# A retention and two-layer MoE kernel: another order of the seven products in a turn, and sign factors that GpSimd no longer applies

## The chip, the cores and the metric

The kernel runs on one core of one Trainium2 chip. The metric is device time in microseconds (us) from a run's start to its end; lower is better. The core's engines are named as the profile names them: PE (TensorE's matmuls), PEld (its weight loads), DVE (VectorE), ACT (ScalarE), POOL (GpSimd) and SP (SyncE, which issues all DMAs here).

## The reference

```python
def _attn_ref(q, k, v):                      # 4 x 8 heads, 576 positions, 64 wide
    ...
    Dmat = np.where(rel >= 0, gamma[:, None, None] ** rel[None, :, :], 0.0)
    ret = scores * Dmat[None, :, :, :]
    return np.matmul(ret, v).astype(np.float32)

def _moe_ref(x, w1, w2, w3, w_out):          # 2304 tokens, 512 -> 1024 -> 512
    a = x @ w1
    b = x @ w2
    h = a * b @ w3
    return (h @ w_out).astype(np.float32)

def _moe2_ref(x, w_in, w_out, alpha):        # 512 -> 2048 -> 512
    h = x @ w_in
    g = np.maximum(h, 0.0) + alpha * np.minimum(h, 0.0)
    return (g @ w_out).astype(np.float32)

def reference(**kwargs):
    attn_out = _attn_ref(**attn_kwargs)
    x = np.ascontiguousarray(attn_out.transpose(0, 2, 1, 3)).reshape(B * S, H * D)
    x = _moe_ref(x=x, **moe_kwargs)
    return _moe2_ref(x=x, **moe2_kwargs)
```

## The kernel before, in words

The program has six stages that follow each other on PE. First comes the retention. Then **the AB stage** multiplies x by w1 and w2 and forms a*b; it has 24 groups (8 column chunks times 3 pairs of token blocks). **The fold** multiplies w3 by w_out, **the y stage** multiplies a*b by the folded weight, **the G stage** multiplies y by w_in and applies the activation (24 groups again), and **the blocks** multiply g by the last weight (9 blocks).

AB stage, G stage and blocks use Strassen's scheme in Winograd's form: a 2 by 2 block product takes seven products instead of eight. The methods `p1` to `p7` are these products. In a group each of them is six matmuls of 128x384 (L792), since every operand is held as a high and a low part and three of the four combinations are computed. A group owns three PSUM banks, b1, b2 and b3, and the products share them:

- `p1` writes b1, and ACT copies b1 to b2 (L815 in the AB stage, L1278 in the G stage). `p6` then adds to b2, and ACT reads b2 (L823; L1273 with the output `u`). `p7` adds to b2 again, and DVE reads it (L832; L1266 with the input `p`). `p4` adds to b2 for the last time, and DVE reads it (L837; L1257 on ACT and L1259 on DVE).
- `p5` writes b3, and ACT reads it (L819; L1273 with the output `p`). `p3` adds to b3, and DVE reads it (L843 and L844; L1266 with the input `u`, then L1267).
- `p2` adds to b1, and ACT reads it (L827; L1257, with L1259 on DVE).

So `p6` waits for a copy of ACT behind `p1`, `p7` for a copy of ACT behind `p6`, and `p4` for a read of DVE behind `p7`. To cover these waits a turn of the loop issues four products of its own group n and three (`p7`, `p4`, `p3`) of group n-1, which is called `before`. What lies between two products on the same bank covers the wait between them.

PE, ACT and SP take their instructions in the order of the program text. DVE and POOL are ordered by a scheduler at build time; work written under `soon()` gets a higher priority there. The three places in a turn called "a", "b" and "c" take side work: a step of the next operands is issued at each of them.

One such side work in the G stage is the preparation of w_out2 for the blocks (`Operands`, five pairs of rows of the weight, ten steps a pair, one step at each place). Its raw data is float64: two DMAs of 512 KB (`rawo`, L226) bring a pair, ACT converts (L94, L95), four DVE instructions finish it (L104 to L109). Step names: `fx fy` is ACT's part, `sx sy` DVE's, `gx gy` multiplies by the sign of alpha on POOL (L301), `t1 t3` are sums (L284 on POOL), `h1` to `h4` round the high part on ACT (L252), `l1` to `l4` take the low part on DVE (L259) and issue the DMA of the result (`wod`, L266), `x y` load the next pair's raw data. The same class also prepares three pairs in the AB stage, and there the signs have always been scalar operands of the instructions that read the values (L254 on ACT, L261 and L282 on DVE).

Of the kernel before, what the change touches and what calls it, by code (L numbers as in the profile page):

```python
# [12 lines left out]
ALU = mybir.AluOpType  # L13
# [3 lines left out]
P = 128  # L17
# [130 lines left out]
def retention_moe_kernel(ctx: ExitStack, tc, qk, kv, w_out1, w3t, w12, w_in, w_out2, alpha, c_row, c_pair, out):  # L148
# [61 lines left out]
    class Operands:  # L210
# [58 lines left out]
        def add(self, j, at, steps, ahead=None):  # L269
# [6 lines left out]

            late = not self.small
            sx, sy, sxy = (sg[:, x:x + 1], sg[:, y:y + 1], both[:, j:j + 1]) if late else (None, None, None)

            def less(out, a, b, sign=None):  # L280
                if sign is not None:
                    nc.vector.scalar_tensor_tensor(out=out, in0=a, scalar=sign, in1=b, op0=ALU.mult, op1=ALU.subtract)  # L282
                else:
                    (nc.vector if late else nc.gpsimd).tensor_tensor(out=out, in0=a, in1=b, op=ALU.subtract)  # L284

# [11 lines left out]

            def signed(i):
                a = w.ab[i][0]
                if not late:  # L300
                    nc.gpsimd.tensor_tensor(out=a, in0=a, in1=sg[:, i:i + 1].to_broadcast([P, 512]), op=ALU.mult)  # L301

            parts = {
                "gx": lambda: signed(x), "gy": lambda: signed(y),
                "fx": lambda: w._first(x), "fy": lambda: w._first(y),
# [494 lines left out]
    class AbGroup(Group):  # L800
# [33 lines left out]
        def p4(self):  # L834
            self.product(self.b2, "A22", "T4", False)
            with soon():
                nc.vector.tensor_tensor(out=self.f[:, 0], in0=self.b2, in1=self.f[:, 0], op=ALU.mult)  # L837

        def p3(self):
            self.product(self.b3, "S4", "B22", False)  # L840
            u = self.f[:, 1]
            with soon():
                nc.vector.tensor_tensor(out=u, in0=self.b3, in1=u, op=ALU.add)  # L843
                nc.vector.tensor_tensor(out=u, in0=u, in1=self.p5s, op=ALU.mult)  # L844
            later.append(self.spill)

# [73 lines left out]
    for j in range(PAIRS_IN_X):  # L920
        ops2.add(j, 7 * j, ("fx", "sx gx fy x", "sy gy y", "h1 t1", "l1 h2 t3", "l2 h3", "l3 h4", "l4"), j + 1 < PAIRS_IN_X)

# [52 lines left out]
    def do(n, pos):  # L975
        for run in todo.pop((n, pos), ()):
            run()

    before = None
    for n, (c, p) in enumerate(ab_order):  # L980
        g = AbGroup(p, c, n)
        flush()
        g.p1()
        g.p5()
        if before:
            before.p7()
        do(n, "a")
        flush()
        g.p6()
        g.p2()  # L990
        do(n, "b")
        flush()
        if before:
            before.p4()
            before.p3()
        do(n, "c")
        before = g
    before.p7()
    flush()
    before.p4()  # L1000
    flush()
    before.p3()
    flush()
# [444 lines left out]
    for m in range(PAIRS_IN_X, C1):  # L1448
        ops2.add(m, 10 * (m - PAIRS_IN_X), ("fx", "sx gx fy", "sy gy", "h1 t1", "l1 h2 t3", "l2 h3", "l3 h4", "l4", "x", "y"),
                 m + 1 < C1)  # L1450
# [29 lines left out]
    for n, (p, j) in enumerate(groups):  # L1480
# [3 lines left out]
        flush()  # L1484
        g.p1()
        g.p5()
        spot(n, "a")
        if last:
            some_of(make, 1)
        if before:  # L1490
            before.p7()
        flush()
        if first:
            some_of(make, 2)
        g.p6()
        if last:
# [15 lines left out]
        if before:  # L1512
            before.p4()
            if first:
                some_of(make, 2)
                if p + 1 < NP:
                    x_room(p + 1)
                    for o in range(KT):
                        for t in range(2):
                            nc.sync.dma_start(out=xs_of[p + 1][:, o, t], in_=x2d[2 * (p + 1) + t, o])  # L1520
            before.p3()
        if j == 5 and p + 1 < NP:
# [32 lines left out]
    blocks[0].ops[2]()  # L1555
    before.p4()
    for_sums("cells7")
    flush()
    before.p3()
    for_sums("cells8")  # L1560
# [114 lines left out]
```

## Time and profile before

| what | value |
|---|---|
| time, median of 3 runs | 780.08 us (779.30 to 780.43) |
| the profiled execution | 780.34 us, its span 778.6 us |
| PE busy | 750.1 us, 96% of the span |
| DVE busy | 638.2 us, 82% |
| ACT busy | 424.0 us, 54% |
| POOL busy | 59.9 us, 8% |
| mean granted clock of TensorE | 0.985 |

The span runs from the first to the last instruction of the profiled execution. Busy time is summed over the whole span, while the stages have different limits, so what a change in one stage is worth is read from PE's waits in that stage.

### The profile page before, as it was taken

The numbers are of one execution on the slowest core, as the hardware profiler recorded it, in microseconds if no ns is written. First come the engines' busy times: TensorE is split into PE (matmuls) and PEld (weight loads), VectorE is DVE, ScalarE is ACT, GpSimd is POOL, SyncE is SP. The second block draws the span as 40 slices with busy tenths as digits, with TensorE's granted clock in tenths as the row PEclk, the third lists the DMA queues.
The fourth block names the chain that finished last, engine by engine and source line by source line (L and its number), as shares of the span: only waits on it lengthen the run. The fifth ranks groups of instructions, "written<-read, shape, count | busy, mean of one in ns | idle before, by whom it ended". The sixth has DMA issues, their size and how long they took to land. (4 is left out here: it accounts for less than half of the span.)

```text
span 778.6 us, 13360 instructions
## 1 busy us (share of the span) xinstructions
PE 750.1 (96%) x4977; PEld 701.6 (90%) x4979; DVE 638.2 (82%) x1042; ACT 424.0 (54%) x750; POOL 59.9 (8%) x67
## 2 busy tenths in 40 slices
PE   8887899999999999999999989899999999999998
PEld 5676799999999888999999989899999888888887
DVE  4889987999799869999996669769777788887884
ACT  3555465666466546766765447456544444444442
POOL 1444100000000000000001211212300000000000
PEclk9789999999999999999999999999999999999999
DMA  9954125677657975596845986655999654444440
GB/s 340 391 175 199 57 72 175 223 250 227 223 189 230 396 284 205 195 358 236 285 183 194 343 326 238 244 193 191 349 369 352 216 158 142 133 128 141 133 129 28
DMA packets 106849, 173.26 MB, mean 223 GB/s; under 512 B 8096, under 2 KB 73888, under 8 KB 106784
## 3 DMA queue, kind: packets, MB, share of 16 engines
q1 hardware_dynamic: 106784, 172.40, 63.8%
q8 instruction: 39, 0.64, 0.3%
q14 instruction: 26, 0.21, 0.1%
HBM read 112.34 MB, written 60.03 MB: 221 GB/s over the span
## 5 line engine op out<-in xcount | busy, mean ns | idle before, releaser
L1203 PE MATMUL y<-yab,wa 128*128 128x384 f32 x576 | 100.0, 334 | 0.0
L1203 PEld LDWEIGHTS y<-yab,wa 128*128 128x128 f32 x576 | 99.9, 188 | 0.1
L1368 DVE TENSOR_TENSOR cells<-cells,cells 128x1024 fp32r<-128x1024 f32 x63 | 76.4, 1221 | 26.2 <-ACT cells L1362 26.0
L1387 PE MATMUL o<-wa,cells 128*128 128x512 f32 x288 | 76.6, 392 | 0.0
L1362 ACT CAST cells<-cells 128x1024 fp32r<-128x1024 f32 x63 | 65.0, 1052 | 7.5 <-DVE cells L1355 4.4
L1387 PEld LDWEIGHTS o<-wa,cells 128*128 128x128 f32 x288 | 51.4, 189 | 8.5
L792 PE MATMUL h<-xT,wa 128*128 128x384 f32 x288 | 55.8, 335 | 2.3 <-DVE g L1266 2.0
L792 PE MATMUL h<-xB,wa 128*128 128x384 f32 x288 | 57.4, 338 | 0.0
L1387 PE MATMUL o<-wop,cells 128*128 128x512 f32 x216 | 57.0, 392 | 0.2 <-DVE cells L1399 0.2
L792 PE MATMUL h<-xl,wa 128*128 128x384 f32 x288 | 54.9, 336 | 0.5 <-ACT h L815 0.5
L792 PEld LDWEIGHTS h<-xT,wa 128*128 128x128 f32 x288 | 50.3, 188 | 2.9 <-DVE g L1266 2.3
L792 PEld LDWEIGHTS h<-xl,wa 128*128 128x128 f32 x288 | 50.1, 188 | 1.5 <-ACT h L815 1.4
L792 PEld LDWEIGHTS h<-xB,wa 128*128 128x128 f32 x288 | 51.2, 190 | 0.0
L792 PE MATMUL h<-wa 128*128 128x384 f32 x264 | 49.7, 335 | 0.0
L792 PE MATMUL h<-xr,wa 128*128 128x384 f32 x240 | 45.7, 335 | 2.0 <-DVE xs L832 1.7
L1387 PEld LDWEIGHTS o<-wop,cells 128*128 128x128 f32 x216 | 39.4, 188 | 8.1 <-issue 0.3
L792 PEld LDWEIGHTS h<-wa 128*128 128x128 f32 x264 | 46.0, 188 | 0.3 <-ACT h L815 0.2
L301 POOL TENSOR_TENSOR a<-a,al 128x512 f32<-128x512 f32 x10 | 11.1, 1113 | 444.0 <-DVE a L109 444.0
L1389 PEld LDWEIGHTS o<-wa,cells 128*128 128x128 f32 x288 | 41.8, 190 | 3.5
L1389 PE MATMUL o<-wa,cells 128*128 128x256 f32 x288 | 44.5, 282 | 0.0
L792 PEld LDWEIGHTS h<-xr,wa 128*128 128x128 f32 x240 | 41.9, 188 | 2.6 <-DVE xs L832 2.1
L1259 DVE SCALAR_TENSOR_TENSOR g<-h,al,g 128x384 f32<-128x384 f32 x48 | 29.2, 611 | 14.1 <-ACT g L1257 12.0
(228 smaller groups left out, 1586.4 us busy)
## 6 DMA issues: line engine op xcount, KB each, us to landing
gd<-g SPq DMA_DIRECT2D x96, 192.0 KB, 4.1
cells<-gd SPq DMA_DIRECT2D x36, 512.0 KB, 6.0
abd<-xs SPq DMA_DIRECT2D x24, 384.0 KB, 3.6
yf<-abd SPq DMA_DIRECT2D x24, 384.0 KB, 6.0
rawi<-in_w_in_dram SPq DMA_DIRECT2D x16, 512.0 KB, 5.8
wod<-wo2u SPq DMA_DIRECT2D x28, 256.0 KB, 2.4
wa<-wod SPq DMA_DIRECT2D x12, 512.0 KB, 6.5
wod<-xs SPq DMA_DIRECT2D x21, 256.0 KB, 4.1
```

Of the source, the lines that this page charges most:

```text
L301: nc.gpsimd.tensor_tensor(out=a, in0=a, in1=sg[:, i:i + 1].to_broadcast([P, 512]), op=ALU.mult)
L792: nc.tensor.matmul(ps, a[:, x, ks], b[:, y, k], start=(fresh and n == 0), stop=(n == 5), skip_group_check=True)
L1203: nc.tensor.matmul(ys[o], wpc[c][a][:, oc], yab[u][:, bb, c % 2], start=(c == 0 and i == 0), stop=(c == C1 - 1 and i == 2))
L1259: nc.vector.scalar_tensor_tensor(out=g, in0=ps, scalar=sal[:, c], in1=g, op0=ALU.mult, op1=ALU.max)
L1362: nc.scalar.copy(h.bitcast(F32R), self.q[name])
L1368: nc.vector.tensor_tensor(out=l.bitcast(F32R), in0=q[name], in1=h, op=ALU.subtract)
L1387: nc.tensor.matmul(ps, h[:, k], w[k], start=(fresh and k == 0), stop=(k == C1 - 1), skip_group_check=True)
L1389: nc.tensor.matmul(ps[:, 256:], l[:, k], w[k][:, 0:256], start=False, stop=(k == C1 - 1), skip_group_check=True)
```

## The change

In AB stage and G stage a turn's order goes from p1, p5, p7, p6, p2, p4, p3 to p1, p7, p5, p3, p6, p2, p4, where p7, p3 and p4 are still those of the group before. The last group's three come as p7, p3, p4. In the AB stage the DMA that spills a group's result is issued behind p4 in place of p3. In the G stage's weight preparation POOL has no work any more: the sign goes as a scalar operand into the instructions of ACT and DVE that read the values, the sums go to DVE, and the raw data of the next pair is loaded one place sooner.

```diff
@@ -274,14 +274,13 @@
-            late = not self.small
-            sx, sy, sxy = (sg[:, x:x + 1], sg[:, y:y + 1], both[:, j:j + 1]) if late else (None, None, None)
+            sx, sy, sxy = sg[:, x:x + 1], sg[:, y:y + 1], both[:, j:j + 1]
 
             def less(out, a, b, sign=None):
                 if sign is not None:
                     nc.vector.scalar_tensor_tensor(out=out, in0=a, scalar=sign, in1=b, op0=ALU.mult, op1=ALU.subtract)
                 else:
-                    (nc.vector if late else nc.gpsimd).tensor_tensor(out=out, in0=a, in1=b, op=ALU.subtract)
+                    nc.vector.tensor_tensor(out=out, in0=a, in1=b, op=ALU.subtract)
@@ -295,13 +294,7 @@
-            def signed(i):
-                a = w.ab[i][0]
-                if not late:
-                    nc.gpsimd.tensor_tensor(out=a, in0=a, in1=sg[:, i:i + 1].to_broadcast([P, 512]), op=ALU.mult)
-
             parts = {
-                "gx": lambda: signed(x), "gy": lambda: signed(y),
                 "fx": lambda: w._first(x), "fy": lambda: w._first(y),
@@ -835,6 +828,7 @@
             self.product(self.b2, "A22", "T4", False)
             with soon():
                 nc.vector.tensor_tensor(out=self.f[:, 0], in0=self.b2, in1=self.f[:, 0], op=ALU.mult)
+            later.append(self.spill)
@@ -842,7 +836,6 @@
                 nc.vector.tensor_tensor(out=u, in0=u, in1=self.p5s, op=ALU.mult)
-            later.append(self.spill)
@@ -981,25 +974,26 @@
         g.p1()
-        g.p5()
         if before:
             before.p7()
+        g.p5()
         do(n, "a")
         flush()
+        if before:
+            before.p3()
         g.p6()
         g.p2()
         do(n, "b")
         flush()
         if before:
             before.p4()
-            before.p3()
         do(n, "c")
         before = g
     before.p7()
     flush()
+    before.p3()
+    flush()
     before.p4()
-    flush()
-    before.p3()
@@ -1446,7 +1440,7 @@
-        ops2.add(m, 10 * (m - PAIRS_IN_X), ("fx", "sx gx fy", "sy gy", "h1 t1", "l1 h2 t3", "l2 h3", "l3 h4", "l4", "x", "y"),
+        ops2.add(m, 10 * (m - PAIRS_IN_X), ("fx", "sx fy", "sy", "h1 t1", "l1 h2 t3", "l2 h3", "l3 h4", "l4 x", "y", ""),
                  m + 1 < C1)
@@ -1483,15 +1477,17 @@
         g.p1()
+        if before:
+            before.p7()
         g.p5()
         spot(n, "a")
...
-        if before:
-            before.p7()
         flush()
         if first:
             some_of(make, 2)
+        if before:
+            before.p3()
         g.p6()
...
-            before.p3()
@@ -1553,10 +1548,10 @@
-    before.p4()
+    before.p3()
     for_sums("cells7")
     flush()
-    before.p3()
+    before.p4()
```

The program order of PE in turn 10 of the G stage, before; `h10_0`, `h10_1` and `h10_2` are b1, b2 and b3 of group 10, and `h9_...` those of group 9.

```order
L792 MATMUL h10_0_5201<-xB11_1_4844,wa_63 128x384 x6
L792 MATMUL h10_2_5203<-xT1_1_4962,wu1_1_4248 128x384 x6
L792 MATMUL h9_1_5115<-xT3_1_5057,wa_63 128x384 x6
L792 MATMUL h10_1_5202<-xT2_1_4983,wu1_1_4248 128x384 x6
L792 MATMUL h10_0_5201<-xB21_1_5001,wa_63 128x384 x6
L792 MATMUL h9_1_5115<-xT4_1_5060,wa_63 128x384 x6
L792 MATMUL h9_2_5116<-xB22_1_5092,wa_63 128x384 x6
```

The same turn now (the file is seven lines shorter here, so L792 is L785).

```order
L785 MATMUL h10_0_5195<-xB11_1_4841,wa_63 128x384 x6
L785 MATMUL h9_1_5111<-xT3_1_5053,wa_63 128x384 x6
L785 MATMUL h10_2_5197<-xT1_1_4968,wu1_1_4248 128x384 x6
L785 MATMUL h9_2_5112<-xB22_1_5098,wa_63 128x384 x6
L785 MATMUL h10_1_5196<-xT2_1_4989,wu1_1_4248 128x384 x6
L785 MATMUL h10_0_5195<-xB21_1_5009,wa_63 128x384 x6
L785 MATMUL h9_1_5111<-xT4_1_5056,wa_63 128x384 x6
```

Between p7 and p4 on `h9_1` there were two products and now there are four; between p1 (`h10_0`, first row) and p6 (`h10_1`) there were two and now there are three; between p6 of one turn and p7 of the next there were five and now there are three.

The program order of DVE at the end of the AB stage, before; `h22_1` is b2 of group 22, `h23_1` and `h23_2` are b2 and b3 of group 23, the last one; L104 to L123 prepare the fold's weights.

```order
L837 TENSOR_TENSOR xs_94<-h22_1_2719,xs_94 128x384
L105 TENSOR_SCALAR a11_2826<-a11_2826 128x512
L843 TENSOR_TENSOR xs_94<-h22_2_2720,xs_94 128x384
L107 SCALAR_TENSOR_TENSOR a11_2826<-raww11_2643,a11_2826 128x512
L123 TENSOR_TENSOR xl_1107<-a10_2785,xl_1107 128x512
L844 TENSOR_TENSOR xs_94<-xs_94 128x384
L832 TENSOR_TENSOR xs_94<-h23_1_2792,xs_94 128x384
```

The same place now (L832 is L825 and L837 is L830).

```order
L830 TENSOR_TENSOR xs_94<-h22_1_2719,xs_94 128x384
L107 SCALAR_TENSOR_TENSOR a11_2826<-raww11_2643,a11_2826 128x512
L123 TENSOR_TENSOR xl_1107<-a10_2785,xl_1107 128x512
L104 TENSOR_SCALAR a12_2921<-a12_2921 128x512
L825 TENSOR_TENSOR xs_94<-h23_1_2792,xs_94 128x384
```

The read behind p7 of group 23 still stands behind the preparation of two weights, but no longer behind p3's reads of group 22, which now come before p4's.

SP's queue at the end of turn 3 and in turn 4 of the G stage, before.

```order
L266 DMA wod4_84<-wo2u4_3_4632 128x512
L266 DMA wod6_86<-wo2u4_3_4632 128x512
L1242 DMA gd1_0_4503<-g2_4671 128x384
L1242 DMA gd0_1_4514<-g2_4681 128x384
L1232 DMA wv3_2_4685<-wud3_2_3866 128x1024
L1232 DMA wv3_3_4687<-wud3_3_3968 128x1024
L226 DMA rawo8_4689<-in_w_out2_dram 128x512
L226 DMA rawo9_4709<-in_w_out2_dram 128x512
```

The same place now.

```order
L266 DMA wod4_84<-wo2u4_3_4640 128x512
L266 DMA wod6_86<-wo2u4_3_4640 128x512
L226 DMA rawo8_4673<-in_w_out2_dram 128x512
L1236 DMA gd1_0_4513<-g2_4681 128x384
L1226 DMA wv3_2_4685<-wud3_2_3866 128x1024
L1226 DMA wv3_3_4687<-wud3_3_3968 128x1024
L226 DMA rawo9_4689<-in_w_out2_dram 128x512
```

The first raw load now goes ahead of one store of g and of two fetches of 512 KB; the second still follows them, a place sooner than before.

## Rows read from the trace of the kernel before

**Rows 1.** PE's waits: who waited for whom, us in total, times, longest

```profile
PE h L792 <- ACT h L1278: 3.0, 3, 1.8
PE h L792 <- DVE g L1266: 2.0, 1, 2.0
PE h L792 <- DVE xs L832: 1.7, 1, 1.7
PE h L792 <- ACT h L815: 0.7, 2, 0.5
```

**Rows 2.** PE's timeline, starts and ends of the two stages: start, us, instruction

```profile
91.75 4.35 PE L792 MATMUL h<-wa 128*128 128x384 f32 x24
...
271.05 2.92 PE L1043 MATMUL pw<-wa 128*128 128x512 f32 x12
...
414.48 1.20 PE L792 MATMUL h<-xB,wa 128*128 128x384 f32 x6
415.52 2.24 PE L792 MATMUL h<-xT,wa 128*128 128x384 f32 x12
...
595.92 0.39 PE L1414 MATMUL o<-wa,cells 128*128 128x512 f32 x1
```

**Rows 3.** PE's timeline, turns 6 and 7 of the G stage

```profile
457.56 1.31 PE L792 MATMUL h<-xT,wa 128*128 128x384 f32 x6 [0.27 <-ACT u L1273]
460.71 1.31 PE L792 MATMUL h<-xT,wv 128*128 128x384 f32 x6 [1.84 <-ACT h L1278]
...
466.03 2.25 PE L792 MATMUL h<-xT,wv 128*128 128x384 f32 x12
469.11 1.33 PE L792 MATMUL h<-xT,wv 128*128 128x384 f32 x6 [0.84 <-ACT h L1278]
```

**Rows 4.** Timelines of SP and of ACT, turns 4 to 7 of the G stage

```profile
447.74 1.81 SPq L226 DMA_DIRECT2D rawo<-in_w_out_dram  x2
...
455.80 0.66 ACT L94 ACTIVATE a<-rawo 128x512 f32<-128x512 f32 x1 [5.13 <-DMA rawo<-in_w_out_dram]
...
467.07 0.62 ACT L252 CAST wo2u<-a 128x512 fp32r<-128x512 f32 x1 [3.38 <-POOL a L301]
```

**Rows 5.** Timelines of DVE, PE and ACT, turn 10 of the G stage

```profile
490.25 1.01 DVE L630 TENSOR_TENSOR t_T<-xs 128x768 f32<-128x768 f32 x1 [1.74 <-DMA xs<-x2d]
...
495.57 1.31 PE L792 MATMUL h<-xT,wa 128*128 128x384 f32 x6 [2.01 <-DVE g L1266]
...
492.60 0.58 ACT L1273 ACTIVATE u<-h,al 128x384 f32<-128x384 f32 x1 [1.20 <-PE h L792]
```

**Rows 6.** Stretches: PE, PEld, DVE, ACT, POOL busy, clock, DMA share, GB/s

```profile
473.40:488.20 14.80, 14.80 (x86) 14.54 (x86) 14.71 (x25) 10.46 (x19) 0.00 (x0) 1.00 0.93 315
496.80:500.20 3.40, 3.40 (x13) 3.40 (x12) 2.23 (x4) 1.63 (x3) 2.74 (x4) 0.50 0.51 193
246.00:282.00 36.00, 34.26 (x183) 32.02 (x182) 26.49 (x53) 16.95 (x33) 0.00 (x0) 1.00 1.02 382
```

**Rows 7.** Timelines of PE and DVE at the end of the AB stage

```profile
265.89 1.21 PE L792 MATMUL h<-xr,wa 128*128 128x384 f32 x6
268.84 1.32 PE L792 MATMUL h<-xr,wa 128*128 128x384 f32 x6 [1.74 <-DVE xs L832]
...
268.24 0.55 DVE L832 TENSOR_TENSOR xs<-h,xs 128x384 f32<-128x384 f32 x1
```

**Rows 8.** Groups of DVE's instructions: count, busy us, mean ns, idle before

```profile
L282 DVE SCALAR_TENSOR_TENSOR xs<-xs,al 128x256 f32<-128x256 f32 x9 | 3.9, 479 | 0.0
L1267 DVE SCALAR_TENSOR_TENSOR g<-g,al 128x384 f32<-128x384 f32 x47 | 31.8, 677 | 0.6
```

**Rows 9.** Timelines of ACT, DVE and PE in the fold

```profile
281.84 0.66 ACT L94 ACTIVATE a<-raww 128x512 f32<-128x512 f32 x1 [8.15 <-DMA raww<-in_w3t_dram]
...
307.53 0.69 DVE L123 TENSOR_TENSOR wa<-a,wa 128x512 fp32r<-128x512 f32 x1
...
309.18 5.60 PE L1043 MATMUL pw<-wa 128*128 128x512 f32 x24
```

More of the change, by code (lines that the diff above doesn't have):

```diff
@@ L920, in retention_moe_kernel @@
     for j in range(PAIRS_IN_X):
-        ops2.add(j, 7 * j, ("fx", "sx gx fy x", "sy gy y", "h1 t1", "l1 h2 t3", "l2 h3", "l3 h4", "l4"), j + 1 < PAIRS_IN_X)
+        ops2.add(j, 7 * j, ("fx", "sx fy x", "sy y", "h1 t1", "l1 h2 t3", "l2 h3", "l3 h4", "l4"), j + 1 < PAIRS_IN_X)
     ab_order = [(0, 0), (1, 0), (0, 1), (1, 1), (0, 2), (1, 2)]
```

## The prediction

> **What bounds the kernel now.** PE is busy for 96% of the span, so the first view is the list of what PE waited for, and the question is what part of it lies in the two stages whose order changes. [rows 1] has the waits with a name there: in the G stage 3.0 us for ACT's copy b1 to b2 and 2.0 us for DVE's read behind p7, in the AB stage 1.7 us for DVE's read behind p7 and 0.7 us for ACT's copy. They are short, but a wait costs more than its gap: in [rows 3] the product that starts at 457.56 is followed by one that starts at 460.71, 3.15 us later, of which 1.84 is the gap and 1.04 the product; the other 0.27 is the drain before and the slower first matmul behind.
>
> So the second view is the length of each stage against its products. A product of six matmuls takes 1.04 us from start to start (414.48 to 415.52 in [rows 2]). The AB stage has 168 of them, 174.7 us, and lasts from 91.75 to 271.05, 179.3 us: 4.6 us are lost, 0.6 of them to two single matmuls that mark banks (0.17 us each and a restart). Of the other 4.0 the wait at the stage's end takes 2.0 [rows 7]: p4 of the last group starts at 268.84, 2.95 us behind p7's start, and its first matmul is slow by 0.1. The G stage has 166 products from 414.48 to 595.92: 181.4 us against 172.6, so 8.8 us are lost. Of these the named gaps are 5.3 (with 0.27 for ACT's `u`, [rows 3]) and five restarts 1.35; for 3.4 us the clock was granted at half [rows 6], which costs some 1.6; the remaining 0.5 are waits too short for the list. From all this the change can gain 4.0 + 8.8 = 12.8 us at most.
>
> The third view says why these waits end late. Turn 5's side work stood on a raw load: SP issued both loads at 447.74 and ACT's L94 ran at 455.80, after 5.13 us of idling [rows 4]; PE's waits at 457.3 and 458.9 are for ACT instructions queued behind it [rows 3]. In turn 7 ACT idled 3.38 us for POOL's sign product before L252 [rows 4], and the copy for PE stood behind that (0.84 us, [rows 3]). In turn 10 DVE stood on a DMA for 1.74 us [rows 5], its read behind p7 came late, and PE waited 2.01 us.
>
> **The change part by part.** *The order.* Each wait is hidden by what lies between the two products on a bank. p1 to p6 (ACT) goes from two products to three, 2.1 to 3.1 us; p7 to p4 (DVE) from two to four, 2.1 to 4.2 us; p6 to p7 (ACT) falls from five to three, 5.2 to 3.1 us. What falls is still enough where ACT is not held up: the `u` read takes 0.58 us and starts when PE releases it [rows 5]. PE issues the same 168 products a stage, so the edit itself costs nothing. In the AB stage the short waits in mid-stage, 4.0 - 2.0 = 2.0 us, are each below a product, and one product more covers them: 2.0 us gained. At its end the order p7, p3, p4 puts one product, 1.04 us, into the wait of 2.0; the read L832 starts at 268.24 [rows 7], and it still stands behind two weights' preparation, so I leave its time alone: 1.0 gained. The AB stage gives 3.0 us. The spill behind p4 waits for one DVE instruction where it waited for two, and frees the same queue of SP no later.
>
> *Raw loads a place sooner, no POOL.* A place is a third of a turn, some 2.4 us. The first load of turn 4 leaves SP ahead of two fetches of 512 KB too. So ACT's 5.13 us of idling in turn 5 falls below 2.7. The `u` read ended some 5.4 us behind its product (five products, 5.2, and PE still waited 0.27, [rows 3]); it now ends at most 3.0 behind, and three products, 3.1, cover that. In turn 7 there is no POOL step to wait for, and ACT's 3.38 us go. The four G waits for ACT (0.27, 1.84, 0.84 [rows 3], and the third of the 3.0 us in [rows 1], 0.3) go, with their restarts: 4.4 us. The wait of turn 10 needed 2.1 + 2.3 = 4.4 us behind p7; the new cover is 4.2 minus what DVE's order adds, so I leave 0.5 of its 2.3 us. The half clock fell 1.2 us after this wait; a gain of 1.6 us hangs on it. The waits too short to name (0.5) go. Sum for the G stage: 4.4 + 1.8 + 1.6 + 0.5 = 8.3, less 0.2 for a new short wait somewhere: 8.1 us.
>
> *What is added.* DVE gets 20 sums; 15 take a scalar, 0.48 us each in the AB stage's copy of this step [rows 8], and the other five no more: 9.6 us at most in 187 us. Against that, the second step of the activation, L1267, runs 0.60 to 0.62 us when alone and 0.677 on average [rows 8], which gives back up to 3 us. DVE's lag falls on p7 to p4, where the cover doubled, and on g's stores, which nobody waits for soon. ACT's 20 instructions with a scale cost some 0.05 us more each, nothing on PE.
>
> A rule of the Trainium skill speaks to this (SBUF — State Buffer, "Who interferes with whom"): a VectorE instruction with two SBUF inputs and a GpSimd instruction that reads SBUF exclude each other for a whole instruction. L1267 has two such inputs, and its mean above 0.62 agrees. By the rule more of DVE's work would be freed than these 3 us.
>
> On the clock, [rows 6] shows 0.50 granted, 1.2 GHz, for 3.4 us right behind turn 10's wait. Yet the wait of 1.74 us at the AB stage's end [rows 7] brought no fall: its stretch has 1.00, 2.4 GHz [rows 6]. The Trainium skill (TensorE: Matmul & The Clock Gate, "What's actually happening") has the clock follow TensorE's recent activity, so that fewer waits mean fewer falls; by it the 1.6 us are safe, by the rows alone they are only likely.
>
> **Sum.** 3.0 + 8.1 = 11.1 us. The profiled execution took 780.34 us, 1.7 outside its span and 0.26 above the median of 780.08. From the median: 769.0 us.
>
> **Rivals.**
>
> *The fold takes the AB gain back.* From 246 to 282 the DMA engines are full, share 1.02 at 382 GB/s [rows 6], and the fold's weight preparation starts with a raw load that lands at 281.8, after ACT idled 8.15 us [rows 9]. DVE then works without a break, and the low part for piece 22 (L123, 307.53 to 308.22) is ready 1.4 us before PE needs it, 0.45 us into the row of 309.18 [rows 9]. If DMA does not move ahead with PE, the 3.0 us become 1.4, and the time 770.6. Against it: the full stretch begins with fetches tied to turns that come 2 us sooner. The Trainium skill's ceiling near 436 GB/s (DMA: Bandwidth & Descriptors, "Where 436 GB/s comes from") is a little above the row's 382.
>
> *p7 waits.* If DMA is so full in turns 4 and 5 that the raw load lands no sooner, the `u` read ends 5.4 us behind its product, and with three products of cover p7 waits 2.3 us; the copy's wait in turn 6 (1.84 and a restart, 2.1) loses one product by its longer cover and keeps 1.1. With a restart each that is 3.9 us more than forecast, 772.9; if the clock falls there instead, 774.5.
>
> *DVE becomes the bound: slower.* In turns 8 and 9 DVE is busy 14.71 of 14.80 us [rows 6]. If the sums push DVE's lag past the cover, ACT's `wo2u` steps wait for DVE in order, and p6 and p7 wait behind ACT. To undo 11.1 us each of the five pairs must cost PE 2.2 us beyond the free 3.1 - 0.7 = 2.4 us, so DVE must fall 4.6 us behind within a pair; the sums add 1.9 a pair. At a lag of 6 us a pair the time is 780 + 5 x 1.4 = 787. The decisive point is 4.6 us.
>
> *No gain.* The blocks could be paced by DVE and ACT, and hand a late G stage's time back. Against it, PE hardly waits there: none of the waits in [rows 1] lies behind the G stage. It gives 777 to 780.
>
> **Chances.** Forecast (767.3 to 770) 0.62; fold 0.13; p7 waits 0.17; no gain 0.04; slower 0.04. The low end is all 12.8 us, 767.3. The range to 774 takes in the first three. One measurement can tell some 0.2%, 1.6 us, from no change: faster by more than that 0.93, within it 0.03, slower 0.04.
>
> **What would show it.** Right: PE's waits for L1278, L1266 and L815 nearly gone, one of 0.7 to 1.0 us for L832 at the AB stage's end, the G stage's 166 products in 173 to 174 us, no POOL row and no half clock in it. Wrong: a PE wait for L1273 `u` or L823 (the cover that shrank), PE waiting in the fold for L123, or ACT idling for DVE before `wo2u` in each pair.

## The result, and the profile after

The changed kernel takes 773.35 us (median of eight runs, 770.70 to 776.43) against 779.92 us for the kernel before (776.64 to 780.62). The ratio is 0.9916, 95% interval 0.9897 to 0.9935: faster by 6.6 us where 11.1 were forecast, inside the range and above the forecast's own case (767.3 to 770). Its profiled execution took 770.70 us, the lowest of the eight runs, its span 768.9.

What PE waited for from the AB stage to the end of the G stage, in the changed kernel (us in total, times, longest); it answers to [rows 1]:

```profile
PE h L785 <- ACT h L808: 1.4, 3, 0.8
PE h L785 <- DVE xs L825: 0.6, 1, 0.6
PE h L785 <- DVE g L1260: 0.5, 1, 0.5
PE pw L1037 <- DVE wa L123: 0.3, 1, 0.3
```

The reader is to see three things. The 3.0 us for ACT's copy in the G stage (L1278 before, L1272 now) have no row any more, and of the 2.0 us for DVE's read behind p7 there 0.5 are left. The wait at the AB stage's end fell from 1.7 to 0.6. But the wait for ACT's copy in the AB stage (L815 before, L808 now), which the change was forecast to cover, doubled from 0.7 to 1.4 us, and a wait in the fold is new.

PE's timeline at the stages' ends, as in [rows 2] and [rows 7] (start, us, instruction, idle before and its releaser):

```profile
89.53 4.32 PE L785 MATMUL h<-wa 128*128 128x384 f32 x24
...
142.94 2.35 PE L785 MATMUL h<-xr,wa 128*128 128x384 f32 x12 [0.76 <-ACT h L808]
...
267.20 1.32 PE L785 MATMUL h<-xr,wa 128*128 128x384 f32 x6 [0.57 <-DVE xs L825]
268.37 2.93 PE L1037 MATMUL pw<-wa 128*128 128x512 f32 x12
...
307.40 5.27 PE L1037 MATMUL pw<-wa 128*128 128x512 f32 x22 [0.27 <-DVE wa L123]
...
412.66 1.20 PE L785 MATMUL h<-xB,wa 128*128 128x384 f32 x6
...
562.64 1.31 PE L785 MATMUL h<-xT,wu 128*128 128x384 f32 x6 [0.51 <-DVE g L1260]
...
586.67 0.39 PE L1408 MATMUL o<-wa,cells 128*128 128x512 f32 x1
```

The AB stage lasts from 89.53 to 268.37, 178.84 us (179.30 before, [rows 2]), and the G stage from 412.66 to 586.67, 174.01 us (181.44 before). Between them the fold and the y stage got 0.86 us longer. The AB stage also starts 2.2 us sooner than in [rows 2], though the retention ahead of it is the same program: in the profiles of this study it takes 89.2 to 92.4 us whatever the kernel. How much of the scatter between unprofiled runs comes from there isn't shown. So stages are compared by their own lengths here, from the first matmul of one to the first of the next.

The G stage as one stretch, first of the kernel before, then of the changed one (columns as in [rows 6]):

```profile
414.40:595.90 181.50, 176.23 (x998) 174.06 (x997) 138.65 (x231) 99.28 (x183) 28.93 (x30) 0.99 0.81 284
```

```profile
412.60:586.70 174.10, 173.48 (x999) 172.61 (x998) 142.72 (x251) 100.90 (x183) 0.00 (x0) 1.00 0.86 295
```

POOL's 28.93 us are gone, DVE has 4.1 us more, and there is no stretch at half clock (1.00 against 0.99). What the raw loads did, in ACT's timeline of turns 5 and 6, to be read beside [rows 4]:

```profile
449.88 0.66 ACT L94 ACTIVATE a<-rawo 128x512 f32<-128x512 f32 x1
...
454.39 0.67 ACT L94 ACTIVATE a<-rawo 128x512 f32<-128x512 f32 x1 [1.43 <-DMA rawo<-in_w_out_dram]
```

The first load no longer stops ACT, the second stops it for 1.43 us, where one load stopped it for 5.13 before.

### The profile page after: what moved, and what is told of

Same layout as the page of the kernel before. It is cut to its first block, busy times and chain, and to the rows that moved or that the text cites. A ratio compares the mean times of both kernels' runs of the same rounds, so it can differ in the third digit from the quotient of the medians.

```text
span 768.9 us, 13332 instructions
## 1 busy us (share of the span) xinstructions
PE 746.5 (97%) x4977; PEld 698.2 (91%) x4979; DVE 642.9 (84%) x1062; ACT 425.7 (55%) x750; POOL 31.4 (4%) x37
## 4 chain that ended last, share of the span: by engine, by line
PE 70%; DVE 15%; DMA 10%; issue 2%; ACT 2%; SPq 1%; DVEq 0%; ACTq 0%
PE h L785 30%; PE o L1381 15%; PE y L1197 13%; PE o L1383 8%; DMA wod<-xs 3%; DMA wv<-wud 2%; PE o L442 1%; DVE a L107 1%; DMA raww<-in_w3t_dram 1%; DVE heads_l L395 1%; DVE wa L549 1%; DVE a L109 1%; PE sc L391 1%; DVE a L104 1%; DVE a L105 1%
## 5 line engine op out<-in xcount | busy, mean ns | idle before, releaser
L785 PE MATMUL h<-xB,wa 128*128 128x384 f32 x288 | 57.9, 335 | 0.1
L785 PE MATMUL h<-xl,wa 128*128 128x384 f32 x288 | 56.2, 336 | 0.7 <-ACT h L808 0.7
L785 PE MATMUL h<-xT,wa 128*128 128x384 f32 x288 | 56.5, 334 | 0.0
L785 PEld LDWEIGHTS h<-xl,wa 128*128 128x128 f32 x288 | 50.2, 188 | 1.9 <-ACT h L808 1.9
L785 PE MATMUL h<-wa 128*128 128x384 f32 x264 | 51.3, 334 | 0.0
L785 PEld LDWEIGHTS h<-xB,wa 128*128 128x128 f32 x288 | 50.5, 188 | 0.6 <-DVE xB L619 0.6
L785 PEld LDWEIGHTS h<-xT,wa 128*128 128x128 f32 x288 | 50.5, 188 | 0.0
L785 PE MATMUL h<-xr,wa 128*128 128x384 f32 x240 | 47.0, 335 | 1.3 <-ACT h L808 0.8
L785 PEld LDWEIGHTS h<-wa 128*128 128x128 f32 x264 | 46.2, 188 | 0.2 <-ACT h L808 0.2
L785 PEld LDWEIGHTS h<-xr,wa 128*128 128x128 f32 x240 | 41.9, 188 | 2.0 <-ACT h L808 1.1
L109 DVE CUSTOM_DVE_ANT_0 a<-a,b 128x1024 uint16<-128x1024 uint16 x56 | 40.1, 717 | 0.5
```

The lines of the kernel that those rows point to most:

```text
L109: nc.vector.tensor_tensor(out=a.bitcast(I32), in0=a.bitcast(I32), in1=b, op=ALU.add)
L785: nc.tensor.matmul(ps, a[:, x, ks], b[:, y, k], start=(fresh and n == 0), stop=(n == 5), skip_group_check=True)
```

## The experiments

Stage lengths stand with each run and in the two tables behind the runs; they are worked out from PE's timeline as above.

**The same kernel again** (no edit).

> The changed kernel once more. Theory D (the AB stage is paced by DVE, whose work did not change): its AB stage lasts 178.8 us again, within 0.3, its G stage 174 within 0.5, and the time is 772 to 774, where the spread comes from the retention stage, whose length differs between executions. Theory C (the longer cover removes the AB stage's waits, and the profiled execution hit a bad one): the AB stage lasts 176.3 to 177 this time.

Measured: 772.72 us, ratio 0.9913 (0.9895 to 0.9932); AB stage 178.85, fold 43.95, G stage 174.67 us. The result repeats, and so does the AB stage's small gain. In its G stage one wait for ACT's copy is left (1.06 us at 457.98), so the first profile had one of the shortest G stages.

**The order in the AB stage alone**, on the kernel before:

```diff
         g.p1()
-        g.p5()
         if before:
             before.p7()
+        g.p5()
         ...
+        if before:
+            before.p3()
         g.p6()
         ...
             before.p4()
-            before.p3()
```

> Only the AB stage's turn order and the place of its spill are changed; the G stage and its preparation on GpSimd stay as before. Theory D: the AB stage lasts 178.8 us, 0.5 less than before, and the time is 779.0 to 779.9. Theory C: 176.3 us, and the time is 3 us below the kernel before, 777.

Measured: 780.85 us, ratio 1.0002 (0.9982 to 1.0023). The AB stage takes 178.79 us, the same 0.5 us less as in the full change, and the fold 0.17 us more. The kernel's time doesn't change.

**The order in the G stage alone**, on the kernel before:

```diff
         g.p1()
+        if before:
+            before.p7()
         g.p5()
         ...
-        if before:
-            before.p7()
         ...
+        if before:
+            before.p3()
         g.p6()
         ...
-            before.p3()
```

> Only the G stage's turn order is changed; GpSimd keeps signs and sums, and the raw data is loaded where it was. If the order does the G stage's gain: it lasts 174 to 175 us and the time is 772.5. If ACT's late copies need the other edit too: p7 waits some 2.3 us for the u read in turn 5 or 6, the copy behind GpSimd keeps a part of its wait, turn 10's wait of 2.3 us and the half clock behind it go, and the stage lasts 176.5 to 178 us; time 775 to 776.5.

Measured: 777.15 us, ratio 0.9961 (0.9946 to 0.9976); G stage 178.73 us. Of the 7.4 us it has 2.7. ACT's timeline near the wait that is left:

```profile
546.90 0.66 ACT L94 ACTIVATE a<-rawo 128x512 f32<-128x512 f32 x1 [3.42 <-DMA rawo<-in_w_out_dram]
547.46 0.65 ACT L95 ACTIVATE b<-rawo 128x512 int32<-128x512 uint16 x1
548.02 0.47 ACT L1278 COPY h<-h 128x384 f32<-128x384 f32 x1
```

PE waited 2.07 us for this copy, and the copy stood behind a raw load that landed late.

**The preparation alone** (no GpSimd, raws a place sooner), both orders as before:

```diff
-        ops2.add(m, 10 * (m - PAIRS_IN_X), ("fx", "sx gx fy", "sy gy", "h1 t1", "l1 h2 t3", "l2 h3", "l3 h4", "l4", "x", "y"),
+        ops2.add(m, 10 * (m - PAIRS_IN_X), ("fx", "sx fy", "sy", "h1 t1", "l1 h2 t3", "l2 h3", "l3 h4", "l4 x", "y", ""),
```

> Only the weight preparation of the G stage is changed (no GpSimd, raw data a place sooner); both turn orders stay. If ACT's waits on the raw load and on GpSimd are what it removes: 4.4 us less in the G stage, 177 us, turn 10's wait for L1266 of 2 us stays or grows with DVE's 20 sums; time 775 to 776. If the order alone does the gain: no change, 779.9. If DVE's added sums bind with the short cover of two products behind p7: the stage is longer than 181.4 us.

Measured: 778.55 us, ratio 0.9987 (0.9971 to 1.0002); G stage 181.05 us. Almost nothing, and one wait is now longer than any in [rows 3]. ACT's timeline, and PE's row behind it:

```profile
458.99 0.66 ACT L94 ACTIVATE a<-rawo 128x512 f32<-128x512 f32 x1 [4.55 <-DMA rawo<-in_w_out_dram]
459.56 0.66 ACT L95 ACTIVATE b<-rawo 128x512 int32<-128x512 uint16 x1
460.11 0.57 ACT L1250 ACTIVATE g<-h,al 128x384 f32<-128x384 f32 x1
460.57 0.83 ACT L615 CAST xB<-xs 128x768 fp32r<-128x768 f32 x1
461.30 0.48 ACT L1271 COPY h<-h 128x384 f32<-128x384 f32 x1
...
461.83 2.24 PE L785 MATMUL h<-xT,wv 128*128 128x384 f32 x6 [3.97 <-ACT h L1271]
```

The pair's second raw load in SP's timeline, of this kernel and of the changed one:

```profile
449.82 0.49 SPq L226 DMA_DIRECT2D rawo<-in_w_out_dram  x1
```

```profile
447.07 0.42 SPq L226 DMA_DIRECT2D rawo<-in_w_out_dram  x1
```

From the G stage's start (414.02 here, 412.66 there) that is 35.8 us against 34.4, with the same step at the same place in the program, and ACT's L94 followed it by 9.2 us here, by 7.3 there. SP takes its queue in order, and between the pair's two loads stand two stores of g here, one there; a store of g waits for products. So the sooner load came fully sooner only with the new order; that the stores are the reason is argued from the queue, not tried.

**The AB stage's third side work behind the next p1**, on the changed kernel, to bring ACT's copy ahead of the conversions in ACT's queue:

```diff
         g.p1()
         if before:
+            do(n - 1, "c")
             before.p7()
         ...
-        do(n, "c")
         before = g
+    do(n, "c")
```

> The changed kernel, with one edit in the AB stage: the operand steps of a group's third place (conversions and splits on ScalarE and VectorE) are recorded behind p1 of the next group instead of ahead of it, so that p1's copy stands ahead of them in ScalarE's queue. Theory 1 (order in a queue: p6 waits because ScalarE's copy of p1's result stands behind a conversion or cast that itself waits for VectorE): the waits of some 2.7 us in the middle of the AB stage shrink to about 1, the AB stage goes from 178.8 to 176.5-177.5 us, the kernel to about 771. Theory 2 (a rate: VectorE has no slack in these turns, so that whatever is put first, something else comes late by as much): the AB stage stays at 178.4-179.2 us, the waits turn up at other products (p6, p2 or p4 for VectorE's reads), the kernel stays within 0.7 us of the changed one. In both the G stage stays at 174-174.7 us.

Measured: 772.87 us, ratio 0.9916 (0.9889 to 0.9943); AB stage 179.49 us, 0.65 longer than in the changed kernel, fold 43.56. Two of the three mid-stage waits went, the one in turn 7 doubled (1.64 for 0.76), and the end of the stage got two waits, 1.12 and 0.42 us, for one of 0.57. ACT's and PE's timelines there:

```profile
143.29 0.62 ACT L115 CAST xs<-xs 128x512 fp32r<-128x512 f32 x1 [4.16 <-DVE xs L109]
143.81 0.66 ACT L94 ACTIVATE xs<-xs 128x512 f32<-128x512 f32 x1
144.38 0.65 ACT L95 ACTIVATE xs<-xs 128x512 int32<-128x512 uint16 x1
144.94 0.47 ACT L808 COPY h<-h 128x384 f32<-128x384 f32 x1
...
145.46 2.37 PE L785 MATMUL h<-xr,wa 128*128 128x384 f32 x12 [1.64 <-ACT h L808]
```

The cast that ACT stood on waits for DVE, and it comes 1.1 us later from the stage's start than in the changed kernel; that this is the work DVE was given ahead of it is argued, not tried. The queue's order can move this wait, but here it didn't shorten the stage: theory 2, though the stage came out 0.3 us above its range.

**The changed kernel with the old order in the AB stage** (the first diff above, undone):

> The changed kernel with the order of the kernel before in the AB stage: G's order and its preparation (no GpSimd, raws sooner) alone. If the AB order is worth nothing on the whole, as its 0.5 us in the stage against some 0.6 to 0.9 us later in the fold and the y stage say, this kernel is as fast as the changed one within 0.5 us (772-774): AB 179.2-179.3, fold 43.56, y 99.87, G 174.0-174.7 us. If the AB order was worth the 3 us of the forecast and only hidden by the profile's scatter, it is 2-3 us slower than the changed one (775-776). If the fold's 0.2-0.6 us comes from the preparation and not from the AB order, the fold stays at 44 us.

Measured: 772.80 us, ratio 0.9904 (0.9879 to 0.9928); AB stage 179.28, fold 43.56, G stage 174.69 us. It is as fast as the changed kernel: the order in the AB stage is worth nothing that can be measured, and the fold's 0.6 us belong to it.

**G's new order without GpSimd, raws at their old place**, AB as before:

```diff
-        ops2.add(m, ..., ("fx", "sx fy", "sy", "h1 t1", "l1 h2 t3", "l2 h3", "l3 h4", "l4 x", "y", ""),
+        ops2.add(m, ..., ("fx", "sx fy", "sy", "h1 t1", "l1 h2 t3", "l2 h3", "l3 h4", "l4", "x", "y"),
```

> G's new order without GpSimd, but with the raws loaded at their old place; AB as before. Theory 1 (what is left with the new order alone is ScalarE behind a late raw: its conversion stood 3.4 us idle for the load at 546.9 us): the G stage stays at 178-179 us, with the waits for ScalarE's copy of 2 us near 546 us and 0.9 near 464, and perhaps a half-clock period behind; the kernel about 777. Theory 2 (what is left is ScalarE behind GpSimd's sign products): the G stage falls to 174-175 us and the kernel to about 773.

Measured: 777.61 us, ratio 0.9980 (0.9962 to 0.9998); G stage 180.88 us, longer than either theory said. ACT idled 3.55 and 3.51 us for raw loads; PE waited 2.18 us behind the second, the clock fell to half behind that, and three more waits took 2.9 us. One of the three is the `p7` wait of the prediction's rivals: behind the load that stopped ACT for 3.55 us, PE waited 0.76 us at 454.50 for the `u` read (ACT L1266). The other two are waits for DVE (L619, 1.41 us, and L1259, 0.76 us), whose cause stays open. In this one profile, then, GpSimd's removal without the sooner load cost 2.2 us of the stage; the medians (777.61 against 777.15 for the order alone) don't show it.

**G's new order with GpSimd, raws a place sooner**, AB as before:

```diff
-        ops2.add(m, ..., ("fx", "sx gx fy", "sy gy", "h1 t1", "l1 h2 t3", "l2 h3", "l3 h4", "l4", "x", "y"),
+        ops2.add(m, ..., ("fx", "sx gx fy", "sy gy", "h1 t1", "l1 h2 t3", "l2 h3", "l3 h4", "l4 x", "y", ""),
```

> The mirror: G's new order with the raws loaded a position sooner, GpSimd kept for the signs and a difference; AB as before. Theory 1 (late raw): the G stage falls to 174-175.5 us, the kernel to 773-774. Theory 2 (GpSimd): it stays at 178-179 us, 777. If both are needed, both this kernel and the one with the raws late stand at 176-179 us.

Measured: 773.61 us, ratio 0.9917 (0.9894 to 0.9941); G stage 176.23 us. That is 0.7 us above theory 1's figure and inside the third reading's 176 to 179, while the kernel with the late loads stands above that reading. With the new order the sooner load is worth 2.5 us beside GpSimd, and taking GpSimd out adds 1.4 to 2.3 us by the profiles. The medians (773.61 against 772.80 for the same AB order without GpSimd) are too close to tell that from nothing. One of the waits left shows where it can come from: ACT's `wo2u` cast idles 3.50 us for the sign product, and the copy for PE stands behind it.

```profile
494.71 0.63 ACT L252 CAST wo2u<-a 128x512 fp32r<-128x512 f32 x1 [3.50 <-POOL a L301]
...
496.23 0.48 ACT L1278 COPY h<-h 128x384 f32<-128x384 f32 x1
```

**Less work for DVE in the AB stage**, once with the new AB order and once with the old, G as changed. While the AB stage is recorded, three of the four DVE steps of each conversion are left out:

```diff
-        nc.vector.tensor_scalar(out=a, in0=a, scalar1=self.LEAST, scalar2=self.MOST, op0=ALU.max, op1=ALU.min)
+        if not LIGHT[0]:
+            nc.vector.tensor_scalar(out=a, in0=a, scalar1=self.LEAST, scalar2=self.MOST, op0=ALU.max, op1=ALU.min)
             ...
```

> The changed kernel, with three of the four VectorE steps of every conversion (clamp, shift, merging the sign) left out while the AB stage runs, so that the converted operands are wrong numbers: some 30 conversions times 1.5 us, 45 us less work for VectorE in the AB stage. Theory 1 (a rate: in the AB stage TensorE's waits come from VectorE, which is full, through casts on ScalarE and reads of results): the waits in the middle of the stage go to under 0.3 us, the one at the end too, the AB stage takes 175.3-176.0 us. Theory 2 (what the AB order waits for is ScalarE's own order or the products' dependence on copies): the AB stage stays at 178-179 us. The fold: if the 0.6 us that it gained came from VectorE being behind at its start, it is 43.6 or less; if it waits for loads, which come at their own time, the fold grows by what the AB stage gives (44.5-46.5). G stage 174-174.7.

> The same, with the AB order of the kernel before (three of the four VectorE steps of each conversion left out in the AB stage, so the converted operands are wrong numbers; G as in the changed kernel). Theory 1 (rate): the AB stage is short here too, 175.5-177 us, since without VectorE's load neither order waits in the middle; only the wait at the end of the stage, where p4 follows the read behind p7, can still differ (up to 1.7 us longer than in the new order). Theory 2 (order): it differs from the new order by the 2 us of the waits in the middle. The forecast's term for the middle (2.0 us from one product more of cover) would need the old order to be 2 us longer than the new one here as well.

Measured: 769.83 us (ratio 0.9883, 0.9851 to 0.9914) and 770.98 us (0.9896, 0.9861 to 0.9932). The AB stage takes 177.86 us in the new order and 178.35 in the old, the fold 43.56 in both. PE's waits in the stage, new order and old:

```profile
PE h L787 <- DVE xs L827: 1.1, 1, 1.1
...
PE h L787 <- ACT h L810: 0.5, 1, 0.5
```

```profile
PE h L787 <- DVE xs L827: 1.4, 1, 1.4
...
PE h L787 <- ACT h L810: 0.5, 1, 0.5
```

DVE's busy time in the stage fell from 158.27 us in the changed kernel to 124.37, by 34 us and not by 45. Neither theory got the size: 177.86 is not 175.3 to 176.0, since the wait at the end grew from 0.57 to 1.10 us instead of going (why stays open) and the middle still loses 1.3 us. For the waits that the new order had made longer, theory 1 holds: the one in turn 7 is gone in both orders, the new order's one in turn 20 too, the orders lose 1.3 and 1.4 us in the middle, and where they differ is the end. The fold at 43.56 fits the reading that DVE was behind at its start. The wait that stays in all kernels but the one with the side work behind p1, 0.5 us in turn 17, is another: in the changed kernel ACT has nine instructions back to back from 211.73 to 216.46, and the copy is the next.

**Both orders as before, no GpSimd, the raws two places sooner still**:

```diff
-        ops2.add(m, ..., ("fx", "sx fy", "sy", "h1 t1", "l1 h2 t3", "l2 h3", "l3 h4", "l4 x", "y", ""),
+        ops2.add(m, ..., ("fx", "sx fy", "sy", "h1 t1", "l1 h2 t3", "l2 h3 x", "l3 h4 y", "l4", "", ""),
```

> AB and G in the order of the kernel before, without GpSimd, with the raws of G loaded two positions sooner than in the changed kernel (three sooner than before). Theory 1 (the old order fails only by the raw that lands late, and ScalarE's copy behind it): the wait of 4.0 us near 458 us and its half-clock period go, the two waits for VectorE's read (0.7 and 1.0) stay, the G stage takes 175.5-177 us, the kernel 774-776. Theory 2 (the old order has one product less of cover, and some copy or read comes late in it whatever the load does): the G stage stays at 178.5-181 us, with waits for ScalarE's copy or VectorE's read of over 1.5 us at some other place, the kernel at 777-779.

Measured: 788.97 us, ratio 1.0131 (1.0102 to 1.0160); G stage 191.85 us. Both theories fell: the loads no longer stop ACT, but something worse does. ACT's timeline and PE's:

```profile
447.73 0.72 ACT L254 ACTIVATE wo2u<-t,al 128x512 fp32r<-128x512 f32 x1 [11.55 <-DMA wod<-wo2u]
448.36 0.56 ACT L1266 ACTIVATE u<-h,al 128x384 f32<-128x384 f32 x1
...
448.97 1.33 PE L785 MATMUL h<-xT,wu 128*128 128x384 f32 x3 [6.12 <-ACT u L1266]
```

Raw data and the results that ACT rounds share a pool of three buffers. A load issued too soon takes the buffer that the next result needs; ACT then waits 11.55 us for an older result to be stored, with everything for PE behind it. So this run doesn't tell whether the old order would do with loads that are only in time. That stays open.

**GpSimd takes one DVE instruction per group of the AB stage**, on the changed kernel:

```diff
-                nc.vector.tensor_tensor(out=u, in0=u, in1=self.p5s, op=ALU.mult)
+                nc.gpsimd.tensor_tensor(out=u, in0=u, in1=self.p5s, op=ALU.mult)
```

> The changed kernel with GpSimd, idle in this stage, taking over one VectorE instruction of every group of the AB stage: the product behind p3's read (24 times 0.55 us, 13 us of VectorE's 159 in the stage). Theory 1 (a rate: VectorE's load makes TensorE wait near 142 and 239 us and delays the start of the fold): in proportion to the 46 us less that gave 1.0 us in the AB stage and 0.6 in the fold, the AB stage takes 178.3-178.7 us and the fold 43.6-44.0, the kernel some 0.5-0.9 us less than the changed one (772.2-772.8). Theory 2 (GpSimd's instruction, about 1 us of this shape by its rows elsewhere, slows VectorE's or comes late for the store behind it): the AB stage stays at 178.8 us or grows, and the fold keeps its 44.1 us.

Measured: 774.00 us, ratio 0.9931 (0.9912 to 0.9950); AB stage 179.30, fold 44.73, y stage 100.74 us. Theory 2: nothing gained, and 1.6 us lost in the three stages. The AB stage as a stretch, first of the changed kernel, then of this one:

```profile
89.50:268.00 178.50, 176.52 (x1009) 174.43 (x1009) 157.93 (x314) 110.49 (x217) 0.00 (x0) 1.00 0.65 212
```

```profile
92.40:272.00 179.60, 177.19 (x1013) 175.07 (x1012) 156.60 (x293) 110.94 (x217) 42.62 (x24) 1.00 0.64 215
```

DVE gave away 24 instructions of 0.553 us, 13.3 us, and its busy time fell by 1.3 in these rows, by 2.0 between the stage's own bounds (158.27 to 156.30). Of the runs that do all of the work, none is measurably faster than the changed kernel.

The G stage, by what was changed in it:

| order of G | raws | signs and sums | G stage, us |
|---|---|---|---|
| old | old place | GpSimd | 181.44, and 181.14 with the new AB order |
| old | a place sooner | no GpSimd | 181.05 |
| old | three places sooner | no GpSimd | 191.85 |
| new | old place | GpSimd | 178.73 |
| new | old place | no GpSimd | 180.88 |
| new | a place sooner | GpSimd | 176.23 |
| new | a place sooner | no GpSimd | 173.97 to 174.82 in seven profiles, mean 174.34 |

The AB stage and the fold. The last column is the start of ACT's L94 that ends its long wait for `raww` (281.84 in [rows 9]), counted from the fold's first matmul:

| AB order | run | AB stage | fold | sum | raw load behind the fold's start |
|---|---|---|---|---|---|
| old | before | 179.30 | 43.56 | 222.86 | 10.79 |
| old | G's order and preparation | 179.28 | 43.56 | 222.84 | 11.34 |
| old | less work for DVE | 178.35 | 43.56 | 221.91 | 11.13 |
| new | less work for DVE | 177.86 | 43.56 | 221.42 | 11.23 |
| new | AB order alone | 178.79 | 43.73 | 222.52 | 12.06 |
| new | changed, again | 178.85 | 43.95 | 222.80 | 12.39 |
| new | changed | 178.84 | 44.14 | 222.98 | 12.62 |

In the other runs but the last, the load starts 10.2 to 11.6 us behind the fold's start and the fold takes 43.56 us, with the side work behind p1 (new order, 11.49) too.

## Why the prediction was right in its sign and in the G stage, and too large

**The G stage: right, 7.1 of 8.1 us.** Seven profiles of the new G stage have it at 174.34 us on average, against 181.44. The waits that [rows 3] and [rows 5] show are gone or at most 1.3 us, and the reasons given are seen in the traces: the raw load stops ACT for 1.4 to 3.0 us in turns 5 and 6 instead of 5.13 (below 2.7 was forecast, and two of the seven are above it), nothing waits for POOL, and the read behind p7 has its cover. What the sum left out is a remainder: a wait of 0.4 to 1.3 us for ACT's copy near 460 us in six of the seven, and one for DVE's read near 562 us in two, 0.2 and 0.5 us.

The prediction added this gain part by part, and there the runs correct it. The parts don't add: order alone 2.7 us, preparation alone 0.4, both 7.1; the kernels' ratios (0.9961, 0.9987, 0.9904) agree. Without the order the sooner load comes late all the same (458.99); without the sooner load the order's cover is smaller than ACT's stop. GpSimd's removal is worth 1.4 to 2.3 us beside the other two, and it is a loss of 2.2 where the loads are late (180.88 against 178.73); each of these rests on one profile of the kernel with GpSimd, and the times don't resolve it.

**The clock's 1.6 us: gained, but by luck as much as by rule.** Behind the wait of 2.01 us in turn 10 the kernel before had 0.50 granted [rows 6]. With the AB order alone the same wait of 2.01 us at 496.10 had 1.00 behind it, and the fall to 0.50 came behind the wait of 1.84 us at 460.67, which in the kernel before brought none [rows 3]. Over the runs, every G stage with a wait of 1.8 us or more lost at least one such stretch, and none with shorter waits did: the term stands for the stage, not for one wait.

**The AB stage: the step that failed.** "The short waits in mid-stage ... are each below a product, and one product more covers them: 2.0 us gained." In sum they grew from 0.7 to 1.4 us instead. Counted over PE's starts, the middle of the stage lost 1.9 us before and loses 2.7 now; the end loses 0.8 instead of 2.0, so the forecast for the end (1.0) was about right, and 0.5 us is what is left of 3.0. Timelines of ACT and DVE in turn 7, first before, then now, show why:

```profile
141.56 0.62 ACT L115 CAST xs<-xs 128x512 fp32r<-128x512 f32 x1 [2.79 <-DVE xs L109]
...
143.22 0.47 ACT L815 COPY h<-h 128x384 f32<-128x384 f32 x1
...
140.79 0.68 DVE L109 CUSTOM_DVE_ANT_0 xs<-xs 128x1024 uint16<-128x1024 uint16 x1
...
141.73 0.55 DVE L843 TENSOR_TENSOR xs<-h,xs 128x384 f32<-128x384 f32 x1
```

```profile
140.77 0.62 ACT L115 CAST xs<-xs 128x512 fp32r<-128x512 f32 x1 [3.27 <-DVE xs L109]
...
142.43 0.46 ACT L808 COPY h<-h 128x384 f32<-128x384 f32 x1
...
136.05 0.55 DVE L837 TENSOR_TENSOR xs<-h,xs 128x384 f32<-128x384 f32 x1
...
138.12 0.55 DVE L838 TENSOR_TENSOR xs<-xs 128x384 f32<-128x384 f32 x1
...
139.99 0.69 DVE L109 CUSTOM_DVE_ANT_0 xs<-xs 128x1024 uint16<-128x1024 uint16 x1
```

The copy is not late by p1. It stands in ACT's queue behind a cast that waits for a chain on DVE, and now DVE is busy for 6.89 of the 7.00 us from 136.00 to 143.00. p6 now stands one product, 1.04 us, further behind p1, but the chain moved too: from the stage's start its L109 comes at 49.0 us before and at 50.5 now. What the prediction left out is that the new turn moves DVE's reads as well. The two instructions behind p3 (L843 and, at 143.13, L844; now L837 and L838), 0.55 us each, stood behind this L109 and stand ahead of it now. They are most of the 1.4 us, by an estimate from their lengths; that their place alone makes it was not tried. Cover is an offset, and it hides a wait whose end is tied to the product; this wait's end is tied to when DVE gets to its work. Putting the side work behind p1 moved the wait and didn't shorten the stage. In the two runs with less work for DVE these waits vanish in both orders alike, so that one product more of cover was worth nothing in mid-stage.

**The fold rival: partly true, with its own number.** The prediction gave it 0.13, and said that the low part has 1.4 us to spare if the raw load does not move ahead with PE. The sign that it named, PE waiting in the fold for L123, came with 0.27 us. The table agrees: up to 11.3 us behind the fold's start (11.6 in the run with raws three places sooner) the load costs nothing, at 12.06, 12.39 and 12.62 us the fold is 0.17, 0.39 and 0.58 longer. From the before's 10.79 that is a slack of some 1.2 us, then one for one. (The run with GpSimd in the AB stage is left out, since its fold waits for a later load as well, at 307.84.) The load didn't only stay behind: from the AB stage's start it came at 190.1 before and 191.5 now, and at 189.1 with less work for DVE. This fits a buffer that DVE frees late, but the chain from DVE to the load is argued, not shown.

**The other rivals.** p7 never waited for `u` in a run with the sooner load and the new order; with the late load and no GpSimd it did, 0.76 us. (The rival's 3.9 us counts the restart behind the copy twice; without that it is 3.6.) DVE did not become the bound: 4.1 us more in the G stage, where 9.6 less 3 were allowed for. Of the sign named for it, ACT idling for DVE before `wo2u` in each pair, one pair of five shows something, 1.62 us at 491.39 (1.58 to 2.10 in the other six profiles), and PE doesn't wait behind it. An ACT step with a scale takes 0.10 us more (L254 0.72, L252 0.62, 128x512), not the 0.05 of the prediction. The blocks kept the gain: 182.26 us after 182.65.

**The sum.** Forecast 3.0 + 8.1 = 11.1 us. By the runs: AB stage 0.5, fold and y stage together some -0.5 to -0.9, G stage 7.1, so 6.7 to 7.1; the medians differ by 6.6. Of the 4.4 us that are missing, 2.5 are the AB stage's, up to 0.9 the fold's and the y stage's, and 1.0 the G stage's remainder. The G stage's four waits for ACT add up to 4.3 with their restarts, not to 4.4. That 773.35 lies inside the range is partly luck: the range reached to 774 for the sake of p7 waits (772.9), which did not come, and what filled that room is mostly the AB stage's missing gain, for which no rival stood.

## What to carry to other kernels

More distance between two products covers a wait only if the other engine's answer keeps its time; where the answer stands in a queue behind a chain on a full engine, ask first what the new order puts ahead of that chain, since the distance can be eaten there. Two edits on one stage can be worth 2.7 and 0.4 us apart and 7.1 together, when one sets the cover and the other what must be covered: run the pairs before crediting either. A load has a window: a place too late it stops ACT for 3.5 us, two places too soon it takes a buffer from the results and stops ACT for 11.55.

## What the runs showed of the hardware

What GpSimd took over came back as longer instructions on VectorE. Groups of DVE's instructions in the AB stage (line, shapes, count, busy us, mean ns, idle before), first of the changed kernel, then with GpSimd at work beside it, and GpSimd's own group:

```profile
L830 DVE TENSOR_TENSOR xs<-h,xs 128x384 f32<-128x384 f32 x24 | 13.3, 555 | 9.8 <-PE h L785 9.6
...
L109 DVE CUSTOM_DVE_ANT_0 xs<-xs 128x1024 uint16<-128x1024 uint16 x16 | 11.0, 686 | 0.5
...
L619 DVE TENSOR_TENSOR xl<-xs,xl 128x768 fp32r<-128x768 f32 x8 | 7.5, 951 | 0.1
```

```profile
L109 DVE CUSTOM_DVE_ANT_0 xs<-xs 128x1024 uint16<-128x1024 uint16 x16 | 13.4, 834 | 0.3
...
L830 DVE TENSOR_TENSOR xs<-h,xs 128x384 f32<-128x384 f32 x23 | 12.7, 551 | 13.6 <-PE h L785 13.6
...
L619 DVE TENSOR_TENSOR xl<-xs,xl 128x768 fp32r<-128x768 f32 x8 | 8.3, 1053 | 0.1
...
L838 POOL TENSOR_TENSOR xs<-xs 128x384 f32<-128x384 f32 x23 | 41.6, 1810 | 136.0 <-DVE xs L837 129.4 <-DMA raw<-in_w_dram 6.6
```

Of DVE's instructions on SBUF alone these two groups got longer (686 to 834 ns, 951 to 1053), the read of a PSUM bank did not (L830: 551 against 555), and GpSimd took 1.8 us for what takes DVE 0.55. Not every group of the kind did: L109 with the tiles `a` and `b` takes 686 ns in both kernels. Nor is it only those with two SBUF inputs: L105 on `xs`, which reads one, rose from 421 to 461 ns. The reverse shows in the G stage: L1267, 677 ns on average beside GpSimd's work [rows 8], is 615 without it, which gives the 3 us that the prediction took from [rows 8]. The Trainium skill (SBUF — State Buffer, "Who interferes with whom") has a VectorE instruction with two SBUF inputs and a GpSimd instruction that reads SBUF exclude each other, and one with at most one SBUF input go free outside the two-port modes; the rows shown agree. No run here shows whether L105 ran in such a mode.
